# A new written-out order, upsampling on TensorE for two batches, block-diagonal local attention for batch 1, and bf16 totals

## The chip, the cores and the metric

The kernel runs on one core of a Trainium2 chip. The metric is device microseconds of one execution: 1003.59 us is the median of three runs of the kernel before (1002.15 to 1005.89). The engines are named as in the profile: PE (TensorE matmul), PEld (its weight loads), DVE (VectorE), ACT (ScalarE), POOL (GpSimd) and SP (SyncE, which here only issues DMAs).

## The reference

For each of 8 batches and 8 heads of 576 tokens and 64 dimensions, two attentions are added, and a feed-forward layer follows:

```python
q_d, k_d, v_d = (mean over groups of 4 tokens)(q, k, v)      # 144 pooled tokens
out_up    = repeat(softmax(q_d k_d^T / 8) v_d, 4)            # every pooled row four times
out_local = softmax(where(|i - j| < 4, q k^T / 8, -1e9)) v   # a band of 7 keys per token
x = (out_up + out_local) as [4608 tokens, 512]
h = x @ w_in            # 512 -> 2048
out = (h * cos(h)) @ w_out   # 2048 -> 512
```

The two weights come as 64-bit floats. All results are wanted at about fp32 precision, so an f16 pair (high part, low part) stands for each operand of the big products.

## The kernel before, in words

**The work.** Attention is done in 32 units, one for each batch and pair of heads. A unit loads q, k and the rows of v, forms local and pooled scores on PE in fp32 (lines 889 and 897), does the softmax on DVE, ACT and POOL, transposes the probabilities, multiplies them with v (line 1116 pooled, lines 1131 or 1146 local), and adds the two results. Sums of a row are formed by DVE (line 962), products with the reciprocal by DVE, POOL or ACT (line 969). The sum `xs` of a unit is split into an f16 high part `x0h`..`x3h` and a low part `x0l`..`x3l` (the digit is the tile's place in a ring of 4).

**The feed-forward layer** has 12 tiles of 384 tokens and 16 chunks of 128 hidden columns. A step is one tile and one chunk: `gemm1` (line 1222, 12 matmuls of 384 columns; from tile 4 on line 1247, a scheme with fewer products of 192 columns), then on ACT and DVE the cosine (lines 1292, 1293, 1295, 1296), the split of the result into `gh` (line 1303 or 1304) and `gl` (line 592), and two steps later `gemm2` (line 1322, 9 matmuls of 512 columns). Tiles 0 to 2, the tokens of batches 0 and 1, go through the chunks four at a time, since the weights are still arriving: steps 1 to 4 are tile 0, step 5 is the first of tile 1, which needs all four units of batch 1.

**The weights** are decoded chunk by chunk from 64-bit floats (`w_split`, lines 625 to 639: an absolute value on ACT, a clamp at line 626, a shift at 628 and two merges at 630 and 632 on DVE, a square sum on ACT). `w_total` adds the square sums over partitions on PE (lines 655 and 656, fp32 matmuls with a column of ones and a tiny constant), and scales and splits the chunk into f16 (lines 684 to 687).

**Batches 0 and 1** differ from the rest. Their local probabilities are transposed on PE (line 990) and multiplied in 48 small matmuls a unit (line 1131). From batch 2 on DVE transposes (line 995), four DMAs of 48 KB on SP's queue place the 32x32 blocks on the diagonal of the one tile `diag` (line 1001), and 12 matmuls of 96 columns do the product (line 1146).

**The order.** All work is recorded as operations with an engine, a duration, what they read and write, and in many cases a second engine that could do them. The class `Plan` lays them out as a list schedule: each engine takes the ready operation with the smallest key. Keys come from a backward pass; a table `MOVES` shifts keys (first number) and the choice of engine (second number) for single units, and `FILLS` says how many dummy matmuls (`ident_b` times `ident_b`, line 1474) PE does ahead of an operation. The program is then issued in that order: each engine's queue is in order, and what stands at its head waits for its inputs.

Of the kernel before, what the change touches and what calls it, by code (L numbers as in the profile page):

```python
# [59 lines left out]
NDIAG = 2  # L60
# [12 lines left out]
    "x_scale": {(0,): (-16.6, 0.1), (1,): (30.85, 0), (2,): (0, 1.4)},
    "u_t": {(0, 0): (-32.45, 1.75), (0, 3): (2.3, 0), (1, 2): (0, 5.6), (1, 3): (0, -2.4), (2, 0): (9.95, 0), (2, 3): (0, 4.8), (3, 0): (7.2, 0),
        (3, 3): (-17.65, 0), (4, 0): (0, 3.65), (4, 3): (16.15, 0), (5, 1): (-28.25, 0), (5, 2): (-48.05, 0), (6, 0): (16.95, 0), (6, 2): (8.05, 3.45),
        (7, 0): (-114.1, 8.35)},
    "u_pv": {(0, 0): (1.2, 0.15), (0, 1): (-15.3, 0), (0, 2): (-218.5, 2.2), (0, 3): (-40.2, -0.25), (1, 0): (13.65, 0), (1, 1): (0, -5.05), (1, 2): (43.1, 0),
# [34 lines left out]
FILLS = {
    "u_s": {(0, 1, 0): -4, (0, 2, 0): -4, (0, 3, 1): -4, (1, 0, 0): -4, (1, 1, 0): -2, (1, 1, 1): -1, (1, 2, 0): 3, (1, 2, 1): -4, (1, 3, 0): -2},
    "u_t": {(0, 0, 2): -4, (0, 1, 0): -2, (0, 1, 2): -4, (0, 2, 0): -4, (0, 2, 1): 16, (0, 2, 2): -4, (0, 3, 0): -2, (0, 3, 1): -1, (0, 3, 2): -1, (1, 0, 0): -1,
        (1, 0, 1): -1, (1, 0, 2): -2, (1, 1, 0): 2, (1, 1, 1): -4, (1, 1, 2): -4, (1, 2, 0): -4, (1, 2, 1): -3, (1, 2, 2): -4, (1, 3, 0): 3, (1, 3, 1): -3,
        (1, 3, 2): -4},
    "u_pv": {(0, 0, 0): -1, (0, 0, 1): -2, (0, 1, 1): -4, (0, 2, 0): -1, (0, 2, 1): 5, (0, 3, 0): -1, (0, 3, 1): 2, (1, 0, 1): -4, (1, 1, 0): -4, (1, 1, 1): -2,
        (1, 2, 0): -4, (1, 3, 0): -4, (1, 3, 1): -4},
    "w_split": {('o', 0, 0): 2},
}  # L120
# [1401 lines left out]
```

## Time and profile before

| | |
|---|---|
| median of 3 runs | 1003.59 us |
| the profiled execution | 1002.97 us, its span 1001.2 us |
| PE busy | 933.3 us (93%), 10615 matmul records |
| DVE busy | 802.9 us (80%), 1879 instructions |
| ACT busy | 620.6 us (62%), 1342 instructions |
| POOL busy | 350.3 us (35%), 583 instructions |
| granted TensorE clock, mean over the span | 0.96 of full speed |

Busy time counts what an engine executes, with waits for a port inside an instruction; matmul ends are modelled, so PE at 93% is not PE at its peak. The clock is 1.0 at 2.4 GHz and 0.5 at 1.2 GHz.

### The profile page before, as it was taken

What the parts mean: (1) busy time and instruction counts of PE and PEld (TensorE: products, weight loads), DVE (VectorE), ACT (ScalarE), POOL (GpSimd) and SP (SyncE); (2) the same over time, 40 slices, a digit from 0 to 9 for tenths busy, and PEclk for the clock granted to TensorE, in tenths of its full rate; (3) what the DMA queues carried; (4) which work ended last, traced back from release to release, by engine and by line L of the source; (5) the groups of instructions that cost most, each with busy time, mean ns of one, the idle gap of its engine ahead of it and who ended that gap; (6) DMA issues with size and microseconds to landing.
All of it is one profiled execution on the core that took longest, in us unless ns stands there. A gap on an engine that the chain in (4) does not pass through costs nothing.

```text
span 1001.2 us, 26440 instructions
## 1 busy us (share of the span) xinstructions
PE 933.3 (93%) x10615; PEld 620.1 (62%) x10615; DVE 802.9 (80%) x1879; ACT 620.6 (62%) x1342; POOL 350.3 (35%) x583
## 2 busy tenths in 40 slices
PE   7697999999999989899999999999999999999998
PEld 5575555555555555466676676766666776666765
DVE  7969979799998979979688797676679896755554
ACT  3646676776775556468567675665555756655644
POOL 3313645344654747565122432411123531100000
PEclk7656999999999999899999999999999999999999
DMA  7834784765356722333121351210030220000000
GB/s 227 240 115 134 196 198 147 164 135 141 81 136 142 168 64 58 72 99 109 33 82 33 88 138 47 63 63 23 3 104 26 64 75 9 2 33 1 33 1 32
DMA packets 48195, 89.53 MB, mean 89 GB/s; under 512 B 5768, under 2 KB 22408, under 8 KB 48072
## 3 DMA queue, kind: packets, MB, share of 16 engines
q1 hardware_dynamic: 41592, 73.88, 24.2%
q0 software_dynamic: 6480, 13.96, 9.2%
q8 instruction: 83, 1.36, 0.6%
q14 instruction: 40, 0.33, 0.1%
HBM read 65.01 MB, written 18.09 MB: 83 GB/s over the span
## 4 chain that ended last, share of the span: by engine, by line
PE 52%; DVE 33%; ACT 5%; issue 3%; DMA 2%; POOL 1%; SPq 0%; DVEq 0%; ACTq 0%; POOLq 0%
PE bank L1322 22%; PE bank L1247 18%; PE bank L1222 5%; DVE tr L1296 4%; DVE tr L1293 4%; DVE gl L592 3%; DVE bank L1261 2%; DVE wv L630 2%; ACT tr L1292 1%; PE bank L1146 1%; DVE wv L632 1%; PE bank L889 1%; DVE su L962 1%; PE bank L897 1%; DVE wv L626 1%
## 5 line engine op out<-in xcount | busy, mean ns | idle before, releaser
L1322 PE MATMUL bank<-wo,gh 128*128 128x512 f16 x1152 | 344.2, 381 | 0.4 <-ACT ob L1339 0.4
L1322 PE MATMUL bank<-wo,gl 128*128 128x512 f16 x576 | 218.9, 380 | 0.1
L1292 ACT ACTIVATE tr<-bank,bquart,hs 128x384 int32<-128x384 f32 x144 | 95.8, 667 | 110.8 <-PE bank L1247 86.9
L1322 PEld LDWEIGHTS <-gh 128*128 128x128 f16 x1152 | 107.8, 99 | 85.8 <-issue 4.8
L1261 DVE TENSOR_TENSOR bank<-bank,tr 128x192 f32<-128x192 f32 x192 | 69.3, 361 | 107.5 <-PE bank L1247 104.0
L1247 PEld LDWEIGHTS <-wi 128*128 128x128 f16 x1536 | 129.8, 98 | 24.7 <-issue 6.8
L1295 ACT ACTIVATE tr<-tr,bhalf 128x384 f32<-128x384 f32 x192 | 115.9, 610 | 29.6 <-DVE tr L1293 28.6
L1247 PEld LDWEIGHTS <-room 128*128 128x128 f16 x1152 | 98.6, 98 | 52.4 <-issue 32.2
L1296 DVE SCALAR_TENSOR_TENSOR tr<-tr,rho,bank 128x384 f32<-128x384 f32 x192 | 114.8, 605 | 11.9 <-ACT tr L1295 10.3
L1222 PEld LDWEIGHTS <-wi 128*128 128x128 f16 x768 | 76.1, 100 | 68.1 <-issue 14.8
L592 POOL TENSOR_TENSOR gl<-tr,gh 128x384 f16<-128x384 f32 x45 | 47.7, 1065 | 201.0 <-ACT gh L1303 188.8
L1322 PEld LDWEIGHTS <-gl 128*128 128x128 f16 x576 | 56.4, 98 | 69.1 <-issue 0.8
L1303 ACT ACTIVATE gh<-tr 128x384 f16<-128x384 f32 x154 | 79.9, 520 | 30.8 <-DVE tr L1296 29.4
L1293 DVE SCALAR_TENSOR_TENSOR tr<-bank,hs,tr 128x384 f32<-128x384 f32 x144 | 87.3, 609 | 11.9 <-ACT tr L1292 11.8
L592 DVE TENSOR_TENSOR gl<-tr,gh 128x384 f16<-128x384 f32 x147 | 86.0, 590 | 9.1 <-ACT gh L1303 7.4
L1247 PE MATMUL bank<-room 128*128 128x192 f16 x768 | 79.6, 247 | 12.7 <-DVE bank L1261 12.4
L1257 ACT ACTIVATE tr<-bank 128x192 f32<-128x192 f32 x154 | 49.8, 324 | 43.7 <-PE bank L1247 36.6
L1247 PE MATMUL bank<-room,wi 128*128 128x192 f16 x384 | 42.1, 246 | 0.0
L1010 PE MATMUL bank<-ident,smd 72*72 72x72 f32 x256 | 26.7, 241 | 12.0 <-DVE wh L659 3.5
L1222 PE MATMUL bank<-x3h,wi 128*128 128x384 f16 x128 | 34.4, 336 | 3.8 <-DVE tr L1296 3.0
L1222 PE MATMUL bank<-x1h,wi 128*128 128x384 f16 x128 | 33.8, 326 | 4.2 <-DVE tr L1296 2.6
L889 PEld LDWEIGHTS bank<-k,q 64*32 64x32 f32 x3072 | 31.0, 112 | 10.6 <-issue 6.3
(289 smaller groups left out, 1978.6 us busy)
## 6 DMA issues: line engine op xcount, KB each, us to landing
vl<-vl SPq DMA_DIRECT2D x32, 384.0 KB, 4.4
q<-qT SPq DMA_DIRECT2D x32, 292.0 KB, 3.9
k<-kT SPq DMA_DIRECT2D x32, 292.0 KB, 3.8
out<-ob SPq DMA_DIRECT2D x36, 256.0 KB, 2.4
out<-ob POOLq DMA_DIRECT2D x33, 256.0 KB, 6.0
wd<-w_in SPq DMA_DIRECT2D x16, 512.0 KB
wd<-w_out SPq DMA_DIRECT2D x16, 512.0 KB, 4.3
vsum<-vdn POOLq DMA_DIRECT2D x18, 288.0 KB, 5.1
```

The source lines that it names most:

```text
L592: f = lambda e: lambda: e.tensor_tensor(out=out(), in0=in0(), in1=in1(), op=ALU.subtract)
L889: pe.matmul(banks[h].get()[BS * i:BS * (i + 1), LQ + BS * s:LQ + BS * (s + 1)], q.get()[hs, o:o + BS], k.get()[hs, o:o + BS], start=not ea ...
L1222: pe.matmul(ph.get()[:, :m], w[:, i, kc, :], x[:, kc, :], start=(n == 0), stop=(n == 3 * KC - 1))
L1247: pe.matmul(bk.get()[:, lo:lo + HT], a(i)(kk), bx(j, k)(kk), start=start and n == 0, stop=n == 5, skip_group_check=True)
L1257: pl.op("ACT", _act(HT), lambda: act.activation(t.get(), src(), AF.Copy), r=[bk], w=[t], alts=[("DVE", _dve(HT), lambda: dve.tensor_copy(t ...
L1261: o = pl.op("DVE", _dve(HT), lambda: dve.tensor_tensor(out=out(), in0=src(), in1=hold[i].get(), op=ALU.add), **kw)
L1292: pl.op("ACT", _act(m, True, 2), lambda: act.activation(ti(), h(), AF.Identity, bias=bquart, scale=inv()), r=[ph, also, hs], w=[tr])
L1293: pl.op("DVE", _dvs(m), lambda: dve.scalar_tensor_tensor(out=tr.get(), in0=h(), scalar=inv(), in1=ti(), op0=ALU.mult, op1=ALU.subtract), r ...
L1295: pl.op("ACT", _act(m, False, 1), lambda: act.activation(tr.get(), tr.get(), AF.Sin, scale=2.0 * PI, bias=bhalf), w=[tr], tab="sin")
L1296: pl.op("DVE", _dvs(m), lambda: dve.scalar_tensor_tensor(out=tr.get(), in0=tr.get(), scalar=rho(), in1=h(), op0=ALU.mult, op1=ALU.mult), r ...
L1303: pl.op("ACT", _act(m, False), lambda: act.activation(ghv(), trv(), AF.Copy), r=[tr], w=[gh], alts=[("DVE", _dve(m / 2), lambda: dve.tenso ...
L1322: pe.matmul(o, (gh, gh, gl)[k].get()[:, sl], wo.get()[:, (0, 1, 0)[k]], start=(c == c0 and k == 0), stop=(c == c1 - 1 and k == 2))
```

## The change

It has five parts.

1. The planner knows more: an operation may carry a `port`, and while one of DVE and POOL holds it the other's operation with a `port` starts later; two engines may not be in one PSUM bank at once (`clash`); POOL costs `n*0.0017+0.165` us instead of `n*0.0024+0.15`. `MOVES` and `FILLS` are new tables found with that planner, so the order changes everywhere.
2. In batches 0 and 1 PE adds the pooled result: an identity matmul in fp32 spreads `xd` four times over the two banks (line 1166 of the new kernel), the local matmuls accumulate onto it, and one scaled copy per bank writes `xs` (lines 1203 and 1204), where DVE added from PSUM before (line 1156). High and low parts are then formed as in later batches: the low part by a subtraction that POOL can do too, where it was a scaled DVE instruction before (line 1095).
3. Batch 1 takes the path of batches 2 to 7 (`NDIAG` 1 for 2): transposes on DVE, four DMAs, `diag`.
4. The totals are bf16 matmuls, which read the upper half of each fp32 word.
5. The clamp of `w_split` (line 626, now 664) can go to POOL.

```diff
-NDIAG = 2
+NDIAG = 1
 MOVES = {
-    "u_vd": {(0, 3): (25.85, 0)},
+    "u_vd": {(0, 2): (0, -2.3), (1, 0): (0, 2.5), (1, 3): (-31.95, 0)},
...
 FILLS = {
-    "w_split": {('o', 0, 0): 2},
+    "w_split": {('o', 5, 0): 6, ('o', 6, 0): 5},
...
+            if not back and e in o.port:
+                x = t
+                if lock != e and lock1 > t:
+                    x = lock1 if lockn == 1 else min(lock1, lock0 + (lock1 - lock0) / lockn * (math.floor((t - lock0) * lockn / (lock1 - lock0)) + 1.0))
+                dur += x - t
+                lock, lock0, lock1, lockn = e, x, t + dur, o.port[e]
...
+    top = lambda t: t.bitcast(BF16).rearrange("p (n t) -> p n t", t=2)[:, :, 1]
...
-        pl.op("DVE", 0.335, lambda: dve.tensor_scalar(out=v.get(), in0=v.get(), scalar1=2.0 ** -15, scalar2=F64_TOP,
-                                                    op0=ALU.max, op1=ALU.min), w=[v])
+        clamp = lambda e: lambda: e.tensor_scalar(out=v.get(), in0=v.get(), scalar1=2.0 ** -15, scalar2=F64_TOP, op0=ALU.max, op1=ALU.min)
+        pl.op("DVE", 0.335, clamp(dve), w=[v], alts=[("POOL", _pool(n), clamp(pool))], port=BOTH)
...
-                    pe.matmul(bk.get()[:, z:z + 1], wide(ones), q.get()[:, i:i + 1], start=i == cols[0], stop=False)
+                    pe.matmul(bk.get()[:, z:z + 1], wide(ones), top(q.get()[:, i:i + 1]), start=i == cols[0], stop=False)
...
-            elif b < GRP:
-                f = lambda: xscale[0].get().bitcast(F32)
...
-                pl.op("DVE", _dve(m), lambda hi=hi, src=src, low=low: dve.scalar_tensor_tensor(
-                    out=low(), in0=src(), scalar=f(), in1=hi(), op0=ALU.mult, op1=ALU.subtract), r=[xs, done, xscale[0]], pw=[x_b[tt]])
...
+        if b < GRP:
...
+            def up_mm():
+                for e in range(2):
+                    pe.matmul(slot(e), ident, spread(e), start=True, stop=False, skip_group_check=True)
+            evac(SD, xd.get, lambda: banks[0].get()[:, 2 * SD:3 * SD], banks[0], xd, scale=0.25)
+            xd.w[-1].deps += poo.w
+            lead = [pl.op("PE", 2 * _mm4(S // 2), up_mm, r=[xd], pw=banks, w=[pl.buf(None)], ni=8)]
...
+        if b < GRP:
+            f = lambda: xscale[0].get().bitcast(F32)
+            for e in range(2):
+                pl.op("ACT", _act(S // 2, True, 1), lambda e=e: act.activation(dst(e), src(e), AF.Copy, scale=f()), r=[banks[e], loc[e], xscale[0]], pw=[xs],
+                      alts=[("DVE", _dve(S // 2), lambda e=e: dve.tensor_scalar(out=dst(e), in0=src(e), scalar1=f(), scalar2=None, op0=ALU.mult))])
```

PE's queue in batch 0, at the local products of its first two units, before (`ptl` holds local probabilities, transposed, `smd` pooled ones, `vm` the largest square sums of v):

```order
L1131 MATMUL bank<-ptl,vl 64x24 x48
L990 MATMUL bank<-ident,sml 128x128 x3
L723 MATMUL bank<-ident,vm 128x128
L724 MATMUL bank<-ones,tiny 128x128
L1474 LDWEIGHTS ident_b
L1474 MATMUL bank<-ident_b 128x256
L1010 MATMUL bank<-ident,smd 72x72 x4
L1131 MATMUL bank<-ptl,vl 64x24 x48
```

And now, at the second unit of batch 0:

```order
L1147 MATMUL bank<-ptd,vsum 64x144 x4
L1527 LDWEIGHTS ident_b
L1527 MATMUL bank<-ident_b 128x256
L1048 MATMUL bank<-ident,smd 72x72 x8
L1166 MATMUL bank<-xd,ident 128x288 x2
L1178 MATMUL bank<-ptl,vl 64x24 x48
L1028 MATMUL bank<-ident,sml 128x128 x3
```

The two identity matmuls stand between pooled and local product, and wait for the copy of `xd` out of PSUM. Dummy matmuls (line 1527 now) went from 79 to 260; 235 of them, against 79, stand ahead of step 5.

DVE's queue where the first `xs` of batch 0 is made, before:

```order
L632 SCALAR_TENSOR_TENSOR wv<-wd,wv 128x512
L969 TENSOR_TENSOR smd<-smd,su 72x576
L1156 TENSOR_TENSOR xs<-bank,xd 128x3x96 x2
L626 TENSOR_SCALAR wv<-wv 128x512
L1093 TENSOR_SCALAR x0h<-xs,xs_711 128x384
L1093 TENSOR_SCALAR x1h<-xs,xs_711 128x192
L626 TENSOR_SCALAR wv<-wv 128x512
L1095 SCALAR_TENSOR_TENSOR x0l<-xs,xs_711,x0h 128x384
L628 TENSOR_SCALAR wv<-wv 128x512
L1095 SCALAR_TENSOR_TENSOR x1l<-xs,xs_711,x1h 128x192
```

And now:

```order
L664 TENSOR_SCALAR wv<-wv 128x512
L859 TENSOR_REDUCE qkd<-q 128x144
L1204 TENSOR_SCALAR xs<-bank,xs_980 128x3x96
L666 TENSOR_SCALAR wv<-wv 128x512
L1130 CAST x0h<-xs 128x384
L950 TENSOR_REDUCE mxl<-bank 128x3x2
L630 TENSOR_TENSOR x0l<-xs,x0h 128x384
L630 TENSOR_TENSOR x1l<-xs,x1h 128x192
```

The two additions are one scaled copy here (the other half is ACT's), the clamps have largely left, and the low parts are subtractions.

SP's queue, where the weights of chunks 4 to 6 are loaded, before:

```order
L614 DMA wd<-w_in 128x4x256
L614 DMA wd<-w_out 128x1024
L614 DMA wd<-w_in 128x4x256
L614 DMA wd<-w_out 128x1024
L614 DMA wd<-w_in 128x4x256
L814 DMA q<-qT 128x584
```

And now:

```order
L652 DMA wd<-w_in 128x4x256
L1039 DMA diag_82<-ptl 32x384 x4
L652 DMA wd<-w_out 128x1024
L652 DMA wd<-w_in 128x4x256
L1039 DMA diag_82<-ptl 32x384 x4
L652 DMA wd<-w_out 128x1024
```

Four groups of four `diag` DMAs now stand among the weight loads, ahead of step 5, where none stood.

Over the whole program DVE loses 166 instructions (1881 to 1715) and POOL gains 132 (588 to 720), ACT gains 36 and SP 16.

## Rows read from the trace of the kernel before

**Rows 1.** Stretches: us, busy us (count) of PE, PEld, DVE, ACT, POOL, clock, DMA, GB/s

```profile
0.00:81.50 81.50, 61.70 (x1425) 47.80 (x1426) 66.50 (x169) 39.15 (x128) 23.28 (x55) 0.69 0.66 198
81.50:117.20 35.70, 31.68 (x524) 22.20 (x524) 33.01 (x86) 23.20 (x54) 20.03 (x36) 0.81 0.55 167
117.20:380.80 263.60, 248.73 (x2389) 141.46 (x2388) 238.23 (x547) 179.46 (x355) 141.97 (x222) 0.99 0.59 137
380.80:1001.20 620.40, 591.22 (x6280) 408.64 (x6278) 465.16 (x1082) 378.76 (x809) 165.02 (x272) 0.99 0.18 50
```

**Rows 2.** Timeline where the first product of tiles 0 and 1 begins

```profile
81.66 0.48 PE L1222 MATMUL bank<-x0h,wi 128*128 128x384 f16 x1 [1.32 <-ACT smd L950]
...
117.35 0.33 PE L1222 MATMUL bank<-x1h,wi 128*128 128x384 f16 x1
```

**Rows 3.** Chain of waits, 0 to 120 us: start, us, engine, tile, line, records

```profile
53.37 1.51 PE bank L1116 x8
...
60.79 1.39 PE bank L1474 x6
62.19 2.70 PE bank L1131 x96
...
66.60 0.22 PE bank L655 x2
...
71.70 0.22 PE bank L656 x2
71.92 0.39 PE bank L990 x3
...
83.23 1.43 DVE wv L632
...
87.48 1.55 DVE wv L630
```

**Rows 4.** Single lines on DVE: ns min/median/max, first and last start, shapes

```profile
L1156 DVE TENSOR_TENSOR xs<-bank,xd x16: 438/446/458, 39.1 to 114.7; 128x288 f32<-128x288 f32 x16
...
L1095 DVE SCALAR_TENSOR_TENSOR x1l<-xs,xs,x1h x8: 403/406/420, 42.2 to 116.2; 128x192 f16<-128x192 f32 x8
L1095 DVE SCALAR_TENSOR_TENSOR x0l<-xs,xs,x0h x4: 604/606/659, 41.3 to 66.8; 128x384 f16<-128x384 f32 x4
...
L626 DVE TENSOR_SCALAR wv<-wv x32: 409/416/1056, 35.7 to 262.8; 128x512 f32<-128x512 f32 x32
```

**Rows 5.** Groups of instructions: count, busy us, mean ns, idle before

```profile
L592 DVE TENSOR_TENSOR gl<-tr,gh 128x384 f16<-128x384 f32 x147 | 86.0, 590 | 9.1 <-ACT gh L1303 7.4
L592 POOL TENSOR_TENSOR gl<-tr,gh 128x384 f16<-128x384 f32 x45 | 47.7, 1065 | 201.0 <-ACT gh L1303 188.8 <-DVE gh L1304 11.0 <-PE bank L889 0.7
```

**Rows 6.** Timeline, 86 to 90 us, DVE and POOL

```profile
87.16 1.32 POOL L969 TENSOR_TENSOR smd<-smd,su 72x576 f32<-72x576 f32 x1
87.40 1.63 DVE L630 SCALAR_TENSOR_TENSOR wv<-wd,wv 128x512 int32<-128x512 int32 x1
...
89.89 0.68 DVE L630 SCALAR_TENSOR_TENSOR wv<-wd,wv 128x512 int32<-128x512 int32 x1
```

**Rows 7.** Tile gl on DVE at 300 to 400 us, then at 900 to 1000 us

```profile
L592 DVE TENSOR_TENSOR gl<-tr,gh x14: 510/557/962, 299.8 to 398.6; 128x384 f16<-128x384 f32 x14
...
L592 DVE TENSOR_TENSOR gl<-tr,gh x24: 548/554/559, 901.0 to 993.2; 128x384 f16<-128x384 f32 x24
```

**Rows 8.** Chain of waits and timeline, PE at the full clock

```profile
181.44 1.94 PE bank L1322 x9
...
86.80 1.59 PE L1131 MATMUL bank<-ptl,vl 32*64 32x24 f32 x96
...
307.90 0.71 PE L1116 MATMUL bank<-ptd,vsum 72*64 72x144 f32 x8
308.44 1.16 PE L1146 MATMUL bank<-diag,vl 128*64 128x96 f32 x24
```

**Rows 9.** Line 1001, the DMAs of diag: SP's waits, and times to landing

```profile
L1001 SPq EVENT_SEMAPHORE  x36: 17/22/21389, 277.9 to 836.1; - x36
...
DMA to landing us min/median/max: 1.9/2.3/4.3
```

**Rows 10.** Who waited for whom: us in total, times, longest us

```profile
PE bank L1247 <- DVE bank L1261: 15.5, 33, 1.5
...
PE bank L1222 <- DVE tr L1296: 5.9, 7, 2.7
```

More of the change, by code (lines that the diff above doesn't have):

```diff
@@ L73 @@
[L73 to L77, printed above, removed]
[6 rows of a table removed]
@@ L111 @@
+    "u_v": {(3, 0): (17.6, 0)},
+    "s_make": {(1,): (1.25, -0.7), (2,): (-34.75, -14.2), (3,): (0, -1.25), (4,): (-8.7, 0.1), (5,): (0, -0.4), (6,): (74.45, 0), (7,): (27.3, 0.05)},
+    "v_norm": {(7,): (-102, 0)},
+}
+TURNS = {
 }
 FILLS = {
[L113 to L116, printed above, removed]
@@ L120 @@
+    "u_pv": {(0, 0, 0): -4, (0, 0, 1): 7, (0, 0, 2): -4, (0, 1, 0): 12, (0, 1, 2): -4, (0, 2, 0): -4, (0, 2, 1): 8, (0, 2, 2): 4, (0, 3, 0): 2, (0, 3, 2): -4,
[4 rows of a table added]
 }
 CFG = dict(alttol=0.3, tabpen=3.2, fgap=0.4, f0=0.8, fend=300.0, fstep=0.13, cap=40, beat=3.4133, phase=1.7, low=0.36, up=0.38, relax=((), ("DVE", "ACT", "POOL", "SP")))
-OWN = dict(PE=0.14, ACT=0.1, DVE=0.08, POOL=0.03, SP=0.0)
+OWN = dict(PE=0.14, ACT=0.1, DVE=0.08, POOL=0.13, SP=0.0)
 NBANK = 8
@@ L254, in run @@
         late = {e: {f: late(f, e) if back else late(e, f) for f in self.engines} for e in self.engines}
-        free = {e: 0.58 if e == "SP" and not back else 0.0 for e in self.engines}
+        free = {e: 2.9 if e == "SP" and not back else 0.0 for e in self.engines}
         ready = {e: [] for e in self.engines}
@@ L270, in run, with clash @@
         W = CFG["beat"]
+        lock, lock0, lock1, lockn = None, 0.0, 0.0, 1
+        seen = {b: ({}, {}) for b in self.banks}
+        def clash(o, e):
+            x = 0.0
+            for b in o.banks:
+                for k, d in enumerate(seen[b]):
+                    if k or e == "PE" or b in o.wb:
+                        for f, y in d.items():
+                            if f != e:
+                                x = max(x, y + late[f][e])
+            return x
         def on(pos, work, act):
@@ L370, in run @@
             t = max(t, avail[o][e])
+            if o.banks and e != "PE" and not back:
+                t = max(t, clash(o, e))
             dur = o.alts[e][0]
@@ L428, in run @@
                 for b in o.banks:
+                    seen[b][e == "PE" or b in o.wb][e] = end
                     open_[b] -= 1
@@ L539, in attn_ffn_kernel @@
     bquart, bhalf = const.tile([P, 1], F32, name="bquart"), const.tile([P, 1], F32, name="bhalf")
-    ones, tiny = const.tile([P, 2], F32, name="ones"), const.tile([P, 1], F32, name="tiny")
+    ones, tiny = const.tile([P, 2], BF16, name="ones"), const.tile([P, 1], BF16, name="tiny")
+    top = lambda t: t.bitcast(BF16).rearrange("p (n t) -> p n t", t=2)[:, :, 1]
     wide = lambda t: t[:, 0:1].broadcast_to([P, P])
@@ L821, in u_qk @@
             pl.op("DVE", _dve(S), lambda i=i: dve.tensor_reduce(out=qkd.get()[:, i], in_=s4[i](), axis=AX.X, op=ALU.add),
-                  r=[src], pw=[qkd], alts=[("POOL", 3 * _pool(2 * SD), on_pool)])
+                  r=[src], pw=[qkd], alts=[("POOL", 3 * _pool(2 * SD), on_pool)], port=dict(POOL=3))
         st.setdefault((b, pr), {}).update(q=q, k=k, qkd=qkd, qkg=qkd.get)
@@ L854, in v_add @@
             return f
-        pl.op("POOL", 2.2, v_add(pool), w=[vd, vw], pw=[vsum[b]], alts=[("DVE", 1.1, v_add(dve))])
+        pl.op("POOL", 1.7, v_add(pool), w=[vd, vw], pw=[vsum[b]], alts=[("DVE", 1.1, v_add(dve))], port=dict(POOL=2, DVE=2))
         st.setdefault((b, pr), {}).update(vd=vd, vdg=vo)
@@ L976, in u_s @@
                 alts.append(("ACT", 4 * _act(SD, False, 1), scaled))
-            pl.op("POOL", _pool(size), f(pool), r=[su], w=[sm], alts=alts)
+            pl.op("POOL", _pool(size), f(pool), r=[su], w=[sm], alts=alts, port=BOTH)
         u["sml"], u["smd"] = sml, smd
@@ L1056, in put @@
             pl.op("ACT", _act(m // 2, False), lambda: act.activation(hi(), src(), AF.Copy), r=deps, w=[done], pw=[x_b[tt], bh][:1 + (j > 3)],
-                  alts=[("DVE", _dve(m / 4), lambda: dve.tensor_copy(hi(), src()))])
+                  alts=[("DVE", _dve(m / 4), lambda: dve.tensor_copy(hi(), src()))], port=BOTH)
             sub(m // 2, low, src, hi, r=deps + [done], pw=[x_b[tt], bl][:1 + (j > 3)])
@@ L1151, in u_pv @@
             dst = lambda e: xs.get()[:, 12 * BQ * e:12 * BQ * (e + 1)].rearrange("p (n r) -> p n r", r=4)
-        evac(SD, xd.get, lambda: banks[0].get()[:, 2 * SD:3 * SD], banks[0], xd, scale=0.25)
-        xd.w[-1].deps += poo.w
-        for e in range(2):
+        if b < GRP:
[3 more added lines that the diff above has]
+                      alts=[("DVE", _dve(S // 2), lambda e=e: dve.tensor_scalar(out=dst(e), in0=src(e), scalar1=f(), scalar2=None, op0=ALU.mult))])
+        else:
+            evac(SD, xd.get, lambda: banks[0].get()[:, 2 * SD:3 * SD], banks[0], xd, scale=0.25)
+            xd.w[-1].deps += poo.w
+        for e in range(2 * (b >= GRP)):
             pl.op("DVE", _dve(S // 2), lambda e=e: dve.tensor_tensor(out=dst(e), in0=src(e), in1=up(e), op=ALU.add),
@@ L1178, in mix @@
             f = lambda e: lambda: e.tensor_tensor(out=out(), in0=x(), in1=y(), op=op)
-            pl.op("POOL", _pool(2 * P), f(pool), alts=[("DVE", _dve(2 * P), f(dve))], **kw)
+            pl.op("POOL", _pool(2 * P), f(pool), alts=[("DVE", _dve(2 * P), f(dve))], port=BOTH, **kw)
         def put(i, t, tb):
@@ L1184, in put @@
             pl.op("ACT", _act(2 * P, False), lambda: act.activation(hi(), t(), AF.Copy), r=[tb], w=[d], pw=[st_],
-                  alts=[("DVE", _dve(P), lambda: dve.tensor_copy(hi(), t()))])
+                  alts=[("DVE", _dve(P), lambda: dve.tensor_copy(hi(), t()))], port=BOTH)
             mix(lo, t, hi, ALU.subtract, r=[tb, d], pw=[st_])
@@ L1267, in gemm1s @@
         keep(0, X, x)
-        o = add(lambda: X.get()[:, :HT], y, 0, r=[Y, hold[0]], w=[c11])
+        o = add(lambda: X.get()[:, :HT], y, 0, r=[Y, hold[0]], w=[c11], wb=(X,))
         X.acc.append(o)
@@ L1274, in gemm1s @@
         product(X, HT, lambda l: S(0, l), wsum_t[(p, 0)][0], 3, False, [X])
-        Y.acc.append(add(y, x, 2, r=[X, hold[2]], w=[c22], after=[o]))
+        Y.acc.append(add(y, x, 2, r=[X, hold[2]], w=[c22], after=[o], wb=(Y,)))
         product(X, HT, lambda l: S(3, l), wsum_t[(p, 3)][0], 2, False, [X])
         product(Y, 0, lambda l: A(1, 1, l), wgt[("i", c + 1)], 6, False, [Y])
-        add(z, z, 1, r=[hold[1]], w=[Y])
+        add(z, z, 1, r=[hold[1]], w=[Y], wb=(Y,))
         g_part(t, c, c0, c1, X, lambda: X.get()[:, :TT], *rooms[0], c11)
@@ L1303, in g_part @@
         pl.op("ACT", _act(m, False), lambda: act.activation(ghv(), trv(), AF.Copy), r=[tr], w=[gh],
-              alts=[("DVE", _dve(m / 2), lambda: dve.tensor_copy(ghv(), trv()))])
+              alts=[("DVE", _dve(m / 2), lambda: dve.tensor_copy(ghv(), trv()))], port=BOTH)
         sub(m, glv, trv, ghv, r=[tr, gh], w=[gl])
```

82 lines of the change are left out of this document (47 added, 35 removed), and 67 rows, old and new, of tables (FILLS, MOVES).

## The prediction

> **What bounds the kernel now.** I read the table of stretches first, then the chain of waits in the opening, then single lines on DVE and PE. [rows 1] cut the span where the first product of tile 0 and of tile 1 begin, 81.66 and 117.35 us [rows 2]. To 81.5 us PE runs at 0.69 of its clock, to 117.2 at 0.81; afterwards at 0.99. DVE is busy 66.5 and 33.0 us in these stretches, 99.5 of 117.2, and the chain of waits goes through DVE's weight decoding (L632, L630) and, from 53 to 75 us, through small fp32 work on PE [rows 3]: so the opening is DVE's, with PE's low clock second. From 117 to 381 us PE is busy 248.7 of 263.6 and DVE 238.2: PE bounds, with DVE at 90% close behind. From 381 us PE is busy 591.2 of 620.4 and DVE has room (465.2). PE's idle time is 23.8, 14.9 and 29.2 us in the three parts.
>
> The span is thus the moment at which step 5 starts (117.2 us) plus 884.0 us, of which 839.9 are PE's work and 44.1 its idle time. I forecast both terms.
>
> **The opening, on DVE.** Ahead of the fifth L1293 (the work of step 5) DVE's queue has 263 instructions before and 246 now, counted off the order. Gone are 16 additions L1156 at 0.446 us (-7.1) and 16 scaled low parts L1095, 8 at 0.406 and 8 at about 0.608 (-8.1) [rows 4]; 6 scaled high parts (-2.3); 6 of 12 clamps L626 at 0.416 [rows 4] (-2.5); 4 of 10 products L969 (-2.8); some small scale instructions (-2.2), an output copy and an addition of v (-1.8). New are 5 scaled copies L1204 (+1.5, priced like L1093), 8 subtractions for low parts (+3.8, like L592), 4 high parts (+1.2), 4 transposes L995 (+2.3), and, because the order brings them forward, three more chunks of decoding and split (+6.5), three pooled sums of q and k (+2.2), work of batch 2 (+1.6) and small ones (+1.2). The sum is -6.5 us. For step 1 the same count gives -15: tile 0 starts well earlier, and the order spends part of that on batch 1 and on weights.
>
> **The opening, on PE.** Ahead of step 5 PE gains 16 identity matmuls of 288 fp32 columns. Their price is not shown. [rows 8] have L1116: 8 records of 144 columns in 0.71 us at 2.4 GHz, as many record-columns as one unit's pair has; if the two head halves of L1116 run side by side the pair costs twice that. So 0.7 to 1.4 us for a unit, 1.0 taken, 8 in all, and double at 1.2 GHz. Batch 1's local product becomes 4 x 1.16 for 4 x 1.59 (-1.7) [rows 8], its PE transposes go (-1.6: four times the 0.39 of [rows 3]), 5 output groups of 3 matmuls come forward (15 x 0.216 = 3.2, from 1.94 for 9 [rows 8]), and the scores of one unit of batch 2 (about 1.3). 156 more dummy matmuls stand there: 1.39 for 6 at the low clock [rows 3], so 0.23 each, 0.115 at the high one: 18 to 36 us. They are meant for gaps; work was 61.7 + 31.7 = 93.4 of 117.2 us, nearly all of it stretched by the low clock. If PE's real work, some 57 us at 2.4 GHz by these prices, and 25 us of dummies run mostly at 2.4 GHz, PE needs 82 to 105 us and stays behind DVE. The chain's PE part from 53 to 75 us would shrink too; I count only 0.7 us of that, since the identity matmuls add a round trip PE to ACT to PE in each unit. Step 5 then starts at 117.2 - 6.5 - 0.7 = 110.0 us. ACT gets about 9 us more ahead of it, at 62.4 of 117.2 busy [rows 1]: covered. POOL's new clamp is not shown; its nearest row is the subtraction of 384 columns, 1065 ns mean on POOL against 590 on DVE [rows 5]; with DVE's 0.416 for the clamp as the low end and 1.42 by columns as the high one I take 1.0. With POOL at 43.3 us of 117.2 it has room. Batch 1's four round trips (transpose 0.56, four issues, landing 1.9 to 4.3 [rows 9], product 1.2) take 6 to 9 us each through one `diag`, 24 to 36 in all; step 1 to step 5 leaves about 40.
>
> **After step 5.** PE's work there loses what came forward, 3.2 + 1.3 us, and the totals: 23 matmuls L655 and 17 L656 at 0.22 us for two records [rows 3] become 35 bf16 ones. Bounds for one of these: 0.03 (one column) and 0.22 (no gain); I take 0.1, so 8.8 - 3.5 = 5.3 us (1 to 8). The three later spreads of the maximum, two matmuls each and priced like the totals, save 1.2. Sum 11.0, which leaves 873.0 of the 884.0.
>
> DVE's queue between step 5 and 381 us becomes about 13% lighter by the count (subtractions, L969, output copies and clamps now on POOL or ACT), and PE's waits for DVE are 15.5 us for one line and 5.9 for another [rows 10]. Over the whole span DVE loses about 75 us (166 instructions at their durations). But DVE is not the only thing that holds PE, and POOL's work rises by some 98 us (132 instructions at POOL's durations), which comes back to DVE in part: L630 took 1.63 us where POOL's 1.32 us product ran, 0.68 otherwise [rows 6], and `gl` on DVE reached 962 ns at 300 to 400 us, where POOL is busy, against at most 559 at 900 to 1000, where it is almost idle [rows 7]. So I count 3 us less idle time. 110.0 + 873.0 - 3.0 = 980 us of span. The profiled execution has 1.8 us beside its span, and lies 0.6 us under the median: 982 us.
>
> The Trainium skill speaks against the change here: "SBUF — State Buffer", section "Who interferes with whom", says that VectorE and GpSimd share one pair of ports, and that the second to start is blocked for the first one's whole instruction when VectorE has two SBUF inputs or moves data by a two-port mode. The trace agrees, at the place named above. By that rule alone all 98 us could block DVE; as an estimate from the page, with the half of DVE's work that reads PSUM or reduces left out, 49 us come back of the 75 that leave, DVE stays near 85% from 117 to 381 us, and the sum would be 985.
>
> **The rivals.**
>
> *The clock stays low.* If the dummies don't raise it and the opening runs as stretched as before (93.4 us for 58 us of work and dummies at full rate, 1.6 times), PE needs 82 x 1.6 = 131 us to step 5, 21 later than forecast: 982 + 21 = 1003. For it: the low clock came in long pieces although 79 dummies stood there. Against: three times as many.
>
> *SP's queue is held (slower).* At SP's head a `diag` DMA waits for DVE's transpose, and the weight loads behind it wait too; 23 of 32 loads stand behind the first group. [rows 9] have one wait of 21.4 us at this line. Two such waits cost 30 us where weights are what steps 9 to 33 wait for, none where the seven buffers of `wd` hold SP anyway: 1012 us. It decides when a group is held more than about 8 us with no weight chunk in reserve. Against it: DMA engines are at 0.55 to 0.59 between 81 and 381 us, so loads can catch up.
>
> *The order fits better than counted.* If the lighter DVE takes half of PE's 44 us idle time after step 5, and the chain's PE part shrinks by 5: 982 - 22 + 3 - 5 = 958. By the rule above less would be left of it.
>
> *The change doesn't do what it says.* The planner's durations are off, so that the two engines meet at the port as often as before; POOL's 98 us then cost DVE more, idle time after step 5 stays at 44 and the opening gains only half: 117.2 - 3.6 + 873 + 2 = 989.
>
> **How the numbers follow.** Forecast 982: 0.45; the better fit 958: 0.13; the port as before 989: 0.16; the clock 1003: 0.14; SP 1012: 0.12. What a measurement can tell from no change is 0.5%, 5 us: under 998.6 is faster, over 1008.6 slower. The first three are faster (0.74); the clock rival is "same", as is a tenth of the SP case (0.15); slower is 0.11. The range leaves out half of the 958 case and most of the SP case: 962 to 1006. The cases on the faster side alone span 958 to 993.
>
> **What would show it.** Right: the first product of tile 0 at 65 to 73 us and that of tile 1 at 105 to 114; clock above 0.8 to 81 us; DVE near 730 us busy and POOL near 450; PE idle 38 to 45 us after step 5; L1156 half as frequent in the groups, from 64 to 48. Wrong: a product of tile 1 after 120 us (if with a low clock, the first rival; if PE or SP waits at `diag`, the second), or PE idle over 60 us after step 5.

## The result, and the profile after

The changed kernel takes 970.14 us (median of 4 runs, 967.14 to 973.06); the kernel before took 1002.87 us beside it. The ratio is 0.9676, with a 95% interval of 0.9628 to 0.9723. Timed again later, in six runs, it took 974.54 us, 0.9725 (0.9690 to 0.9759). The forecast was 982, with a range of 962 to 1006. The profiled execution has a span of 971.3 us, against 1001.2 before.

The table of stretches of the changed kernel, cut where the first products of tile 0 and tile 1 begin and where its 57th step begins (steps are the chunks of tiles 0 to 3, four tiles with 16 each; this one began at 380.8 us before), answers to [rows 1]: us, busy us of PE, PEld, DVE, ACT, POOL, clock, DMA share, GB/s.

```profile
0.00:73.80 73.80, 62.03 (x1510) 47.55 (x1511) 57.30 (x143) 38.10 (x126) 47.16 (x80) 0.90 0.68 208
73.80:124.10 50.30, 43.18 (x434) 28.34 (x433) 39.16 (x93) 34.63 (x79) 30.38 (x49) 0.88 0.72 202
124.10:370.20 246.10, 233.48 (x2109) 130.50 (x2108) 215.48 (x472) 173.58 (x344) 154.71 (x224) 0.99 0.58 132
370.20:971.30 601.10, 582.75 (x6416) 407.41 (x6414) 446.63 (x1007) 389.20 (x831) 223.51 (x364) 1.00 0.19 54
sum 971.30, PE 921.44 PEld 613.80 DVE 758.57 ACT 635.51 POOL 455.76; mean PE 230.36 PEld 153.45 DVE 189.64 ACT 158.88 POOL 113.94
```

The timeline of the changed kernel, where tile 0 and tile 1 begin, as in [rows 2]:

```profile
73.91 0.53 PE L1275 MATMUL bank<-x0h,wi 128*128 128x384 f16 x1
...
124.26 0.33 PE L1275 MATMUL bank<-x1h,wi 128*128 128x384 f16 x1
```

Tile 0 begins 7.8 us earlier than before, but tile 1, which I put at 110, begins 6.9 us *later*. By the 57th step the changed kernel is 10.6 us ahead; from there to the end it gains another 19.3. That late part, where I had forecast next to nothing, holds most of the gain. In the profile of the later set, whose span is 971.3 us too, tile 0 begins at 71.9, tile 1 at 121.6 and the 57th step at 367.4, so there the two parts are 13.4 and 16.5 us. To see the late part alone, here is the stretch from the 57th step to the start of the last matmul of `gemm2`, the kernel before first, then the changed one:

```profile
381.00:996.50 615.50, 590.50 (x6279) 408.49 (x6278) 464.30 (x1082) 377.50 (x808) 164.82 (x272) 0.99 0.18 49
```

```profile
370.40:966.60 596.20, 582.05 (x6414) 407.27 (x6413) 445.79 (x1007) 387.95 (x830) 223.31 (x364) 1.00 0.19 53
```

PE is idle 25.0 us of it before and 14.2 after, and is busy 8.4 us less although it does more there (6414 records against 6279). What PE waits for most in this stretch of the changed kernel (engine, line, who released it: us, times, longest):

```profile
PE bank L1193 <- DMA diag<-ptl: 3.8, 2, 2.9
PE bank L1300 <- DVE tr L1311: 1.9, 2, 1.6
PE bank L1193 <- DVE gl L630: 1.5, 1, 1.5
```

The largest wait of before, 15.5 us in 33 pieces for the bank additions [rows 10], isn't there at all. L1261 became L1314, and the products L1247 became L1300.

Groups of the changed kernel (count, busy us, mean ns, idle before), for [rows 4], [rows 5] and the new operations:

```profile
L630 DVE TENSOR_TENSOR gl<-tr,gh 128x384 f16<-128x384 f32 x127 | 77.6, 613 | 10.6 <-ACT gh L1356 7.8
L630 POOL TENSOR_TENSOR gl<-tr,gh 128x384 f16<-128x384 f32 x65 | 65.8, 1014 | 202.6 <-ACT gh L1356 169.6 <-PE bank L1300 15.5 <-issue 12.9
L664 POOL TENSOR_SCALAR wv<-wv 128x512 f32<-128x512 f32 x17 | 35.2, 2073 | 12.4 <-ACT wv L663 10.2 <-ACT mxd L984 1.5
L1209 DVE TENSOR_TENSOR xs<-bank,xd 128x288 f32<-128x288 f32 x48 | 19.9, 446 | 5.5 <-ACT xd L843 5.4
L666 DVE TENSOR_SCALAR wv<-wv 128x512 int32<-128x512 int32 x32 | 15.5, 491 | 8.1 <-POOL wv L664 8.1
L1166 PE MATMUL bank<-xd,ident 128*128 128x288 f32 x32 | 11.5, 484 | 2.8 <-ACT xd L843 1.6 <-ACT ob L1392 1.1
L664 DVE TENSOR_SCALAR wv<-wv 128x512 f32<-128x512 f32 x15 | 7.5, 498 | 1.1 <-ACT wv L663 1.0
```

A clamp on POOL (L664) takes 2.07 us, five times the 0.416 that it takes on DVE [rows 4] and more than the 1.42 that I had as the high end; and DVE's next instruction on the same tile, L666, waits 8.1 us for it in all.

Between the starts of tile 0 and tile 1 the chain of waits runs elsewhere than before. In the kernel before, VectorE holds 25.2 of its 35.7 us there and DMAs nothing; in the changed one DMAs hold 27.8 of 50.4 us (17.8 of 49.7 in the second profile), VectorE 5.4 (10.2). The longest DMA pieces of this chain (start, us):

```profile
86.34 4.07 DMA wd<-w_out
...
90.49 3.79 DMA wd<-w_out
...
94.36 4.33 DMA q<-qT
...
101.90 4.47 DMA wd<-w_in
...
109.21 7.80 DMA vsum<-vdn
```

The DMAs move 10.2 MB between the two starts, where it was 5.9 before.

### The profile page after: what moved, and what is told of

It reads as the page before. It is cut to its first block, busy times and chain, and to the rows that moved or that the text cites. A ratio compares the mean times of both kernels' runs of the same rounds, so it can differ in the third digit from the quotient of the medians.

```text
span 971.3 us, 26178 instructions
## 1 busy us (share of the span) xinstructions
PE 921.4 (95%) x10464; PEld 613.8 (63%) x10464; DVE 758.6 (78%) x1713; ACT 635.5 (65%) x1378; POOL 455.8 (47%) x715
## 4 chain that ended last, share of the span: by engine, by line
PE 65%; DVE 10%; DMA 10%; ACT 6%; POOL 4%; issue 3%; SPq 2%; ACTq 0%; POOLq 0%; DVEq 0%
PE bank L1375 29%; PE bank L1300 20%; PE bank L1275 5%; PE bank L1193 3%; PE bank L927 2%; DMA wv<-vdn 2%; DMA diag<-ptl 2%; PE bank L935 2%; DMA wd<-w_out 1%; SPq L1039 1%; DMA wd<-vdn 1%; DVE tr L1346 1%; PE bank L1147 1%; PE bank L1048 1%; DVE tr L1349 1%
## 5 line engine op out<-in xcount | busy, mean ns | idle before, releaser
L630 POOL TENSOR_TENSOR gl<-tr,gh 128x384 f16<-128x384 f32 x65 | 65.8, 1014 | 202.6 <-ACT gh L1356 169.6
L1300 PEld LDWEIGHTS <-wi 128*128 128x128 f16 x1536 | 129.3, 98 | 23.7 <-issue 5.6
L1314 DVE TENSOR_TENSOR bank<-bank,tr 128x192 f32<-128x192 f32 x192 | 69.0, 361 | 89.4 <-PE bank L1300 82.1
L1300 PEld LDWEIGHTS <-room 128*128 128x128 f16 x1152 | 97.5, 98 | 32.9 <-issue 7.0
L1356 ACT ACTIVATE gh<-tr 128x384 f16<-128x384 f32 x148 | 76.6, 519 | 27.4 <-DVE tr L1349 22.2
L630 DVE TENSOR_TENSOR gl<-tr,gh 128x384 f16<-128x384 f32 x127 | 77.6, 613 | 10.6 <-ACT gh L1356 7.8
L1310 ACT ACTIVATE tr<-bank 128x192 f32<-128x192 f32 x161 | 52.0, 325 | 44.4 <-PE bank L1300 27.3
L1300 PE MATMUL bank<-room 128*128 128x192 f16 x768 | 80.1, 246 | 0.1
L1392 ACT ACTIVATE ob<-bank,os 128x512 f32<-128x512 f32 x63 | 41.4, 680 | 10.5 <-PE bank L1375 9.2
L1300 PE MATMUL bank<-room,wi 128*128 128x192 f16 x384 | 42.1, 246 | 0.0
L1193 PE MATMUL bank<-diag,vl 128*64 128x96 f32 x672 | 34.6, 253 | 7.9 <-DMA diag<-ptl 5.8
L664 POOL TENSOR_SCALAR wv<-wv 128x512 f32<-128x512 f32 x17 | 35.2, 2073 | 12.4 <-ACT wv L663 10.2
L1007 POOL TENSOR_TENSOR sml<-sml,su 128x384 f32<-128x384 f32 x26 | 28.7, 1103 | 26.3 <-DVE su L1005 26.3
```

Source lines behind the costliest of these rows:

```text
L630: f = lambda e: lambda: e.tensor_tensor(out=out(), in0=in0(), in1=in1(), op=ALU.subtract)
L1193: pe.matmul(banks[e].get()[64 * h:64 * h + 64, sg * 4 * BQ:(sg + 1) * 4 * BQ], vt.get()[:, s, :], dg[:, :, s, :BQ], start=b >= GRP, stop=T ...
L1300: pe.matmul(bk.get()[:, lo:lo + HT], a(i)(kk), bx(j, k)(kk), start=start and n == 0, stop=n == 5, skip_group_check=True)
L1310: pl.op("ACT", _act(HT), lambda: act.activation(t.get(), src(), AF.Copy), r=[bk], w=[t], alts=[("DVE", _dve(HT), lambda: dve.tensor_copy(t ...
L1314: o = pl.op("DVE", _dve(HT), lambda: dve.tensor_tensor(out=out(), in0=src(), in1=hold[i].get(), op=ALU.add), **kw)
L1356: pl.op("ACT", _act(m, False), lambda: act.activation(ghv(), trv(), AF.Copy), r=[tr], w=[gh], alts=[("DVE", _dve(m / 2), lambda: dve.tenso ...
```

## The experiments

The theory after reading the two traces: (1) the late gain is bank exclusion, that is, keeping two engines out of one PSUM bank at the same time. From tile 4 on two chunks are done as a pair, in two banks, and VectorE adds parts of one to the other (L1261, now L1314). The first addition of a pair reads one bank and writes another while TensorE has a product to write into the same banks; the planner before let these overlap on paper, and on the chip TensorE waited. The rival (2): it is the lighter VectorE and the new order as a whole. In the plans, the first addition overlaps the next product on its bank in 42 of the 64 pairs of tiles 4 to 11 before, and in none after; there 37 additions stand behind that product and 27 are done ahead of it. Line numbers below are those of each run's own kernel, which its edit shifts by a few lines.

**The addition put back, in the changed kernel (992.55 us, ratio 0.9910, 0.9876 to 0.9945).**

```
+    ...
+    for u, a in adds.items():          # the first addition of each pair
+        m = firsts[u]                  # the next product on its bank
+        if a.start >= m.start and max(p.start for p, _ in a.preds) < m.start - 2e-4:
+            at_[a] = m.start - 1e-4    # all else keeps its place
```

> The changed kernel; in all steps the first bank addition (L1314) that stands behind the next product on its bank is put just ahead of that product; every other instruction keeps its place. Theory 1: TensorE's waits for the addition come back, 8 to 16 us in some 30 pieces, and the time goes from 970 to 978 to 986. Theory 2: VectorE is light enough to do the addition in time, waits under 4 us, time within 3 us of 970.

All 37 were moved, and it cost more than theory 1 said. The same stretch of this kernel, and its largest waits:

```profile
367.60:985.60 618.00, 587.98 (x6414) 408.00 (x6413) 444.78 (x1007) 388.23 (x830) 221.56 (x364) 1.00 0.18 51
```

```profile
PE bank L1302 <- DVE bank L1316: 18.1, 35, 0.9
PE bank L1193 <- DMA diag<-ptl: 3.3, 2, 2.4
```

The stretch is 21.8 us longer, 618.0 against 596.2, and even longer than before. VectorE is as light as in the changed kernel (444.8 us busy), so its lightness alone doesn't remove the wait: theory 2 falls for this order. The stretch is well outside what else was seen: from the 57th step to the last matmul of `gemm2`, the eight profiles of the changed order with the additions in place (the two of the changed kernel and those of six variants below) have 593.7 to 599.3 us, the three of the old order 614.6 to 621.7. One such place in this kernel's timeline (start, us; the wait in brackets), then a like place in the changed kernel:

```profile
712.16 0.38 PE L1379 MATMUL bank<-wo,gl 128*128 128x512 f16 x1
712.99 0.66 PE L1302 MATMUL bank<-room 128*128 128x192 f16 x6 [0.45 <-DVE bank L1316]
```

```profile
705.48 0.38 PE L1375 MATMUL bank<-wo,gl 128*128 128x512 f16 x1
705.70 0.66 PE L1300 MATMUL bank<-room 128*128 128x192 f16 x6
```

Undisturbed, the next product starts 0.22 us after the last matmul of the group ahead; here it starts 0.83 after it. The stop costs 0.61, of which the profile calls 0.45 idle; the other 0.16 is the last matmul running out, by the profile's modelled ends, which otherwise lies under its successor and now counts as busy. 35 stops at 0.16 are 5.6 us, and PE's busy time rose by 5.9 (582.05 to 587.98; by 4.1 against the second profile's 583.85). Taken at every such stop, from start to start against the usual interval, the 35 cost 23.9 us and the 33 of before 21.3, in both 0.17 a stop beyond the wait. So the 33 were worth somewhat more than the 16 to 19 us that the stretch gained (615.5 to 599.2 and 596.2). The Trainium skill, "PSUM — Partial Sum Buffer", section "PSUM bank collisions raise a hardware error", says that the chip itself does not make an engine wait at a shared bank, so the program's order has to keep them apart. No run here shows a collision; the waits here are what keeping apart cost.

**The same place in the kernel before, twice.** First the overlapping additions were put behind the product (42 moved; 1006.19 us, ratio 1.0052, 1.0027 to 1.0076):

```
+        if a.start < m.end and m.start < a.end and last_ > m.start:
+            at_[a] = min(m.end + 0.2, last_)   # last_: just before its first reader
```

> The kernel before; in tiles 4 to 11 the first bank addition (L1261) of a pair of chunks, where its planned time overlaps the next product on the same bank, is emitted behind that product; every other instruction keeps its place. Theory 1 (the gain behind step 5 is the bank: TensorE waited 15.5 us in 33 pieces for these additions): the wait falls under 5 us and the time by 8 to 14 us, to 989 to 995. Theory 2 (the gain comes from the lighter VectorE and the new order as a whole): the wait falls, but other waits take its place, and the time changes by less than 3 us.

Neither theory had this: the waits rose, to 20.4 us.

```profile
PE bank L1249 <- DVE bank L1263: 20.4, 34, 1.7
```

The addition also reads the other bank, which the product behind that one writes; where the two products stand side by side, the wait was only handed on. Of the 34 waits 20 now come directly behind another such product, of the 33 before 6. So the second try also sees to other work between the two (999.99 us, ratio 0.9969, 0.9946 to 0.9993):

```
+        if slot[m2] > slot[m1] + 1 and last_ > m1.start:  # work already between: as above
+        ...
+                at_[m1] = new      # else: the product ahead of the output group
+        ...
+            at_[g] = m2.start - 1e-3   # or: an output group pulled in between
```

> The kernel before; of the 42 pairs of chunks in tiles 4 to 11 whose first bank addition (L1261) overlaps, by the plan, the next product on its bank, 38 are rearranged so that the addition stands behind that product with another group of TensorE's work between it and the product after: 28 by the place of the addition (or of one output group), 10 by moving the product ahead of the output group in front of it. Theory 1 (the two banks of the addition are what TensorE waits for, and the earlier try only handed the wait to the next product, on the other bank): waits at the addition from 15.5 to 2 to 7 us, time 6 to 13 us below the kernel before, 989 to 996. Theory 2 (these waits are slack of the order, and come back elsewhere): 999 to 1005.

```profile
377.40:991.80 614.40, 591.82 (x6279) 408.27 (x6278) 464.42 (x1082) 375.97 (x808) 166.31 (x272) 0.99 0.18 50
```

```profile
PE bank L1249 <- DVE bank L1263: 9.5, 20, 1.0
PE bank L1249 <- DVE tr L1301: 4.8, 3, 4.2
PE bank L1249 <- ACT tr L1259: 3.1, 6, 1.9
```

The wait fell by 6 us, the stretch by 1.1: theory 2 here. By the price of a stop the 13 that went were worth some 8 us. Part came back as waits for ACT's L1259 (3.1 us, not among the waits of this stretch before), and PE's busy time rose by 1.3; the rest isn't settled. So the two orders differ: in the changed one, taking the exclusion away costs what was gained; in the old one, moving instructions by hand at these places recovers almost nothing. That the bank waits are the late gain is thus shown in the changed order alone.

**Both kernels without their tables.** Does the gain need the searched table?

```
-MOVES = { ... }
-FILLS = { ... }
+MOVES, TURNS, FILLS = {}, {}, {}
```

> The kernel before with its tables of shifts and dummies empty, so that its planner sets the order alone: 1030 to 1070 us. With the run beside it this tells what the change's operations and planner rules are worth without a table.

> The changed kernel with its tables empty. Theory 1 (the operations and the planner's rules for lock and bank carry the gain): 15 to 35 us under the kernel before with empty tables, and few waits of TensorE for bank additions. Theory 2 (the gain is in the table that was searched under these rules): the two plain kernels lie within 8 us of each other.

1049.75 us (ratio 1.0472, 1.0444 to 1.0500) and 994.35 us (0.9908, 0.9871 to 0.9944): 55 us between them, more than between the searched ones, and the changed kernel with no table at all is faster than the old one with its table. From the 57th step to the last matmul of `gemm2`, the plain kernel before and its largest waits, then the changed one:

```profile
392.30:1045.60 653.30, 609.29 (x6523) 416.03 (x6521) 483.82 (x1109) 408.28 (x875) 117.11 (x204) 0.98 0.17 49
```

```profile
PE bank L1194 <- DVE bank L1208: 18.4, 39, 2.1
PE bank L957 <- DVE smd L916: 7.8, 6, 2.1
```

```profile
382.30:989.30 607.00, 587.96 (x6519) 408.53 (x6517) 452.56 (x1005) 401.88 (x871) 216.80 (x345) 1.00 0.19 53
```

```profile
PE bank L1237 <- DVE bank L1251: 6.9, 16, 1.2
```

Again the front part gives 10.0 us (392.3 to 382.3) and the late part most: 46.3 us, with the waits for bank additions down from 18.4 to 6.9. Theory 1 of this pair holds, with more than the 15 to 35 us that it expected, though the waits are not few: operations and planner rules carry the gain. It isn't split further: the operations, the lock, the bank rule and the planner's new durations changed together, and by its stops (23 fewer at 0.17, 11.5 us of waits) the bank accounts for some 15 of the 46.

**fp32 totals in the changed kernel (975.11 us, ratio 0.9741, 0.9708 to 0.9775).**

```
-  pe.matmul(bk.get()[:, z:z + 2], wide(ones), top(q.get()), start=True, stop=False)
+  pe.matmul(bk.get()[:, z:z + 2], wide(ones_f), q.get(), start=True, stop=False)
```

and likewise for the other totals and the spreads.

> The changed kernel with the totals of the weights' squares and the spreads of the maximum on fp32 operands again, in the same order. If TensorE's work is the bound behind step 5 and a bf16 record takes 0.03 us where an fp32 one took 0.11 with two records each: TensorE busy 5 to 9 us more, time 4 to 9 us more (974 to 979). Rival: the totals stand in gaps where TensorE waits for weights anyway, and the time grows by less than 2 us.

PE's busy time is 928.6 us, 7.2 more than 921.4, so the size of the term was right. The totals themselves, with count and ns min/median/max, first of this kernel, then of the changed one:

```profile
L696 PE MATMUL bank<-wq,ones_f x64: 166/250/352, 55.7 to 258.1; 128*128 128x1 f32 x64
```

```profile
L693 PE MATMUL bank<-wq,ones x32: 163/165/183, 57.7 to 257.0; 128*128 128x1 bf16 x32
```

But the 57th step began at 370.3 us (370.4 with bf16, 367.4 in the second profile) and the span is 970.8. The time is 0.6 us above the second set of the changed kernel (974.54) and 5.0 above the first, and the intervals overlap. This speaks for the rival, without excluding a few microseconds: the totals, all before 259 us, take time that TensorE would else have spent waiting.

**A third of the dummies (972.92 us, ratio 0.9711, 0.9666 to 0.9756).**

```
-            for _ in range(o.fill if s else 0):
+            for _ in range(o.fill // 3 if s else 0):
```

> The changed kernel with each group of dummy matmuls cut to a third (rounded down; some 80 instead of 260), as many as the kernel before has. Theory 1 (the dummies hold the clock up): granted clock to 124 us from 0.89 to 0.72 to 0.80, the first product of tile 0 from 73.8 to 78 to 84 us, and 2 to 8 us of it left at the end (972 to 978). Theory 2 (the denser real work holds it): clock above 0.85, time within 3 us of 970. A third: the dummies only stand in PE's way, and the time falls.

The first 124.1 us of this kernel, then of the changed one:

```profile
0.00:124.10 124.10, 95.40 (x1767) 66.35 (x1768) 96.38 (x234) 71.30 (x200) 74.90 (x126) 0.77 0.69 202
```

```profile
0.00:124.10 124.10, 105.21 (x1943) 75.89 (x1944) 96.45 (x236) 72.73 (x205) 77.53 (x128) 0.89 0.70 206
```

The dummies do hold the granted clock up, 0.89 against 0.77, and with a third of them tile 0 begins at 82.4 us instead of 73.9 (71.9 in the second profile):

```profile
82.42 0.53 PE L1275 MATMUL bank<-x0h,wi 128*128 128x384 f16 x1
```

That is no earlier than in the kernel before (81.7), although VectorE is as light as in the changed one: tile 0's lead hangs on the dummies. By step 9 the two are 0.9 us apart (137.3 and 136.4; 133.7 in the second profile), and at the end nothing can be measured: theory 1 has the clock right, theory 2 the time.

**The clamps on VectorE, same places (967.90 us, ratio 0.9664, 0.9627 to 0.9702).**

```
-  alts=[("POOL", _pool(n), clamp(pool))], port=BOTH)
+  alts=[("POOL", _pool(n), clamp(dve))], port=BOTH)
```

> The changed kernel with the 17 clamps that it does on GpSimd (2.07 us each) emitted on VectorE instead, at the same places. Theory 1 (the slow clamp delays the weights and blocks VectorE at the shared port): POOL 35 us less, VectorE 7 us more, time 2 to 6 us less (964 to 968). Theory 2 (it is hidden; VectorE at 88% between 124 and 370 us is the scarce one): time the same or up to 5 us more (970 to 975).

```profile
L666 DVE TENSOR_SCALAR wv<-wv 128x512 int32<-128x512 int32 x32 | 14.2, 455 | 0.0
L664 DVE TENSOR_SCALAR wv<-wv 128x512 f32<-128x512 f32 x32 | 13.3, 419 | 2.6 <-ACT wv L663 2.3
```

VectorE does 17 instructions more and is busy 758.9 us, against 758.6: what they take, the others give back (L666 went from 491 to 455 ns). That agrees with the Trainium skill, "SBUF — State Buffer", section "Who interferes with whom", by which either engine can block the other at their shared ports. L666's wait for POOL, 8.1 us in all, is gone too. The 57th step begins at 361.8 us, 8.5 earlier than in the first profile of the changed kernel and 5.6 earlier than in the second. In time, 967.90 against 970.14 and 974.54: theory 1's direction, but the intervals overlap, so a gain of 2 to 7 us isn't settled.

**Batch 1's diagonal DMAs: left out (968.18 us, 0.9654, 0.9624 to 0.9685), then on ScalarE's queue (973.50 us, 0.9705, 0.9683 to 0.9728).**

```
+            if o.eng == "SP" and o.name == "u_t" and o.arg[0] == 1:
+                continue
```

```
-  sp.dma_start(dg[BS * i:BS * (i + 1), i] ...
+  (act if b == 1 else sp).dma_start(dg[BS * i:BS * (i + 1), i] ...
```

> The changed kernel without the 16 DMAs of batch 1 that put its transposed weights on the diagonal (batch 1's local values are then left out of the result; all other instructions stay). Theory 1 (the round trips of these DMAs, and the loads held behind them, are why step 5 begins at 124 and not at 110 us): step 5 begins 8 to 14 us earlier, and the time falls by 3 to 8 us (962 to 967). Theory 2 (the weights are what the steps behind wait for): step 5 moves, step 9 and the end don't; time within 3 us of 970.

> The changed kernel with batch 1's 16 diagonal DMAs issued by ScalarE's queue instead of SyncE's, at the same places of the order. Theory 1 (a diag DMA that waits for VectorE's transpose holds the loads behind it on SP): without that, step 5 begins near 116 us as in the run without these DMAs, and the time is 965 to 970 against 970 to 975 for the changed kernel. Theory 2 (it is the round trip itself, from transpose to landing, that TensorE waits for): step 5 stays at 120 to 125 and the time within 3 us of the changed kernel. ScalarE's own work may be held instead: up to 5 us more.

Tile 1's first product without the DMAs, and with them on ScalarE's queue:

```profile
116.38 0.33 PE L1275 MATMUL bank<-x1h,wi 128*128 128x384 f16 x1
```

```profile
127.90 0.33 PE L1275 MATMUL bank<-x1h,wi 128*128 128x384 f16 x1
```

Without them tile 1 begins 5 to 8 us earlier (121.6 and 124.3 in the two profiles of the changed kernel), step 9 5 to 7 (at 129.1) and the 57th step 4 to 7 (at 363.3), as theory 1 has it, and the chain between tiles 0 and 1 has no DMA in it. All five runs (967.14 to 968.51) lie below the six of the changed kernel that were timed beside them (971.25 to 980.18), 6 us in the medians; against its first set it is 2. Freeing SP's queue doesn't bring this back: holding the loads on SP is not the cause, unless ScalarE's own waits for the DMAs hid that. SP did stand at these DMAs in the changed kernel; its largest waits there, from 60 to 125 us:

```profile
SPq L1039 <- PE bank L1193: 7.9, 2, 6.1
...
SPq L1039 <- DMA wd<-w_out: 5.1, 2, 3.1
```

They are for TensorE's product on the one `diag` and for an earlier load, hardly for VectorE (0.4 us). What these DMAs cost, round trip or traffic, was not told apart.

**The last two together (970.18 us, ratio 0.9678, 0.9647 to 0.9709).**

> The changed kernel with the 17 clamps on VectorE and batch 1's diagonal DMAs on ScalarE's queue. If the two hold step 5 one after the other, the gains add: 959 to 965. If they are one and the same wait (the later of two), 964 to 969, as the clamps alone.

They don't add up: tile 1 begins at 126.5 us, as with the DMAs on ScalarE's queue, and the time lies above both ranges. No complete version here is surely faster than the changed kernel, which was timed again as a control:

> The changed kernel as it is, timed beside the others on one chip: 967 to 974 us, ratio 0.964 to 0.972 by every theory; the runs with one part undone are held against it.

The second set, 974.54 us and 0.9725, lies just above what I gave and within 0.5% of the first; differences under that were read from pairs of profiles or left open.

## Why the prediction was right, and where it was not

The direction, the range and the time to 1.2% were right, but the gain was half as large again as forecast (32.7 us for 21.6), and that the time came out so near is partly luck. Of the three terms of the span, step 5 came 14.1 us late, PE's work behind it was 12.7 less than forecast and its idle time 10.1 less; together they make the 8.7 by which the span is under 980.

- **The opening.** "Step 5 then starts at 117.2 - 6.5 - 0.7 = 110.0 us": it started at 124.3 (121.6 in the second profile), later than the 120 that I had named as wrong. The step that failed is "so the opening is DVE's". I counted VectorE's queue, but behind tile 0 the chain of waits went over to DMAs, whose room I had taken from their mean share ("so loads can catch up"). Ahead of it, tile 0's lead (73.9 us; I had 65 to 73) hangs on the dummies and the clock, at 0.90 as asked, and not on the lighter VectorE alone. PE did not stay behind VectorE either: ahead of step 5 it was busy 105.2 us, VectorE 96.5. Of the 14 us, batch 1's diagonal DMAs, which I let fit into 40 us, took 5 to 8, and clamps at 2.07 us instead of 1.0 another 2 to 4 (tile 1 at 119.9 without them). The rest isn't settled. The mark was badly chosen, too: the new order does more of PE's work ahead of step 5 (105.2 us busy in 124.1, dummies included), and by step 9 both kernels stand at 136. And "nearly all of it stretched by the low clock" misread the rows: with levels of 1.0 and 0.5, means of 0.69 and 0.81 put 62 and 38% of the two stretches at the low one.
- **PE's work.** 839.9 became 816.2 us behind step 5, 23.7 less where I had 11.0: 15.3 up to the 57th step and 8.4 behind it. Some 5 of the 8.4 are the run-out of the stops; how much of the 15.3 is work that the order did ahead of step 5 was not counted. The totals were sized rightly (5.3 with the spreads at 1.2; 7.2 measured for both) and bought no time that could be measured: I put all of PE's work on the path, against my own rows that showed PE idle in that stretch. The identity matmuls came out at the top of their bounds: 11.5 us for 8 units, 1.4 each.
- **Idle time.** "So I count 3 us less idle time" is the other step that failed. It went from 44.1 to 31.0 us. I saw the row [rows 10] with the 15.5 us, and took it for a sign of a busy VectorE, to be relieved a little by lightening it. It was a conflict of two engines over two banks, which the changed plan orders away whole; with the same light VectorE it came back as soon as the additions stood ahead again. With the 0.17 us per stop, that row was worth some 21 us.
- **The rivals.** "The clock stays low" fell (0.90 and 0.88), and the cut dummies show that a clock of 0.77 in the opening cost nothing that could be measured at the end, not 21 us. SP's hold did not make the kernel slower, and it was of another kind than I had named. "The order fits better" took 22 us off the idle time behind step 5, where 13.1 were measured, and for another reason. POOL took over about what I had counted (350.3 to 455.8 us, 98 counted). With each instruction's duration added up, as in my count, VectorE lost 59 us (920.3 to 861.3) where I had 75, so some 16 came back, which is the port's rival in kind. In its busy time, where instructions overlap, it lost 44 (758.6 us; I had 730 as a sign). That rival's 989 us did not follow: TensorE's waits for VectorE behind the 57th step are down to a few single ones. The 49 us that I had estimated from the Trainium skill ("SBUF — State Buffer", section "Who interferes with whom") were too many.

## What to carry to other kernels

A wait that recurs in many short pieces for one line (33 times, 0.5 us each) can be a rule that the schedule doesn't know: look for what the two instructions share before you call it load, and price each stop with its pipeline run-out. Give the planner the constraint rather than mend its output: the changed kernel without any table beat the old one with its table (what its new operations added to that was not told apart), while mending by hand gave 0.3%. Ask again what bounds a stretch once the engine that bounded it is relieved: here it was largely DMAs. And a lead in the opening is worth only what is left of it further on: the dummies' 8.5 us at tile 0 were 0.9 at step 9.

## What was not expected of the hardware

A clamp with two operations, 128x512 fp32, takes a mean of 2.07 us on POOL and 0.42 on DVE in the kernel before, while a subtraction of 128x384 on the two differs only by 1014 against 613 ns. And a break in TensorE's stream costs 0.17 us beyond the idle time that the profile shows (35 breaks: 16 us more idle, 4 to 6 us more busy).
